# A new order of all work items in a two-layer attention and MLP kernel, and half of a matrix in other buffers

## The chip, the core and the metric

The kernel runs on one core of a Trainium2 chip. The core has TensorE (PE, matrix products into PSUM), VectorE (DVE), ScalarE (ACT), GpSimd (POOL) and SyncE (SP, which here issues nearly all DMAs). Each engine works through its own instructions in the order in which the program gives them; semaphores make an instruction wait for data of another engine or of a DMA. The metric is the device time of one execution in microseconds (us), lower is better.

## The reference

The input x is 2048 rows of 448 numbers in f32. Two layers follow each other with the same weights. Each layer is a linear attention block and an MLP block, both with a residual:

```
x = x + A(layernorm(x))          # twice, with B between and after
x = x + B(layernorm(x))

A: q, k, v = x @ wqkv            # 16 heads of 28
   phi(t) = (t + 1 if t > 0 else exp(t)) + 1e-6
   kv = sum over rows of phi(k) v     # per head, 28 x 28
   z  = sum over rows of phi(k)
   out = (phi(q) kv) / (phi(q) z + 1e-6) @ wo
B: gelu(x @ w1 + b1) @ w2 + b2   # 448 -> 1792 -> 448
```

## The kernel before

**Precision.** PE multiplies operands in a rounded format (fp32r). To keep f32 accuracy each operand is split in a high part and a low rest, and a product is made of three: high by high, high by low, low by high. This is why most matmuls come in threes, and why each operand costs a cast (ACT) and a subtraction (DVE or POOL). The last 64 of the 448 columns are packed so that they need two matmuls.

**Tiles and stages.** The rows are 16 tiles of 128. In a layer there are three stages.

*K, Q and G.* For each tile t: `ld` loads x, `a` takes the statistics (DVE), `ar` the root (POOL), `n` normalizes (DVE). The tile is transposed, either on PE (`T`, and `ht` in halves for the first two tiles) or by 32x32 blocks on DVE (`tu`), stored to HBM (`st`) and read back (`sp`), two tiles at a time. `xh` and `xl` split it. `K` and `Q` are 11 matmuls each. `ke`, `kp` apply phi to K (ACT, DVE), `kh`, `kl` split it, `za` adds it up for z (DVE); `qe`, `qp`, `qs` do the same for Q and store it to HBM. `sh`, `sl` split the normalized x as it is, and `G` (11 matmuls) adds up x by phi(k) over all tiles in four PSUM banks.

*From G to the MLP's input.* `z`, `zb`, `dc` make the denominator's vectors, `gt` copies G, `kv` multiplies it by the v weights, `mask` keeps the diagonal heads, and `m` multiplies by `wo`. The result M (448 x 448) is split by `mh`, `ml` in four groups of 112 rows. For each tile `pl` loads phi(q), `pz`, `pd`, `pm` divide it, it is transposed (`pT` on PE for the first four tiles, `pu`, `ps`, `pp` by way of HBM for the others), split (`qh`, `ql`) and multiplied by M: `o` for the first four tiles, `oc` after `mc` has moved M by 14 DMAs to the place of the q weights. `oa` adds it to x, and `la`, `ar`, `ln` normalize for the MLP; `mT` or `mu`, `ms`, `mp` transpose, `yh`, `yl` split.

*MLP.* The rows are four blocks of four tiles, the hidden 1792 columns 14 chunks of 128; a chunk of a block has the number n = 14 x block + chunk, 0 to 55. `f` is the first product of a chunk (11 matmuls of 512 columns), `g` the GELU (ACT), `gh`, `gl` the split (ACT, DVE), `y` the second product (12 matmuls of 448 columns, three for each of the block's tiles; `u` is one tile's three). `ya` adds the block's sums to x, and `ys` stores it.

The weights of the MLP are loaded piece by piece by `bld` and split by `bhi` (ACT) and `blo` (POOL) during the first layer; `wkld`, `wqld` load the k and q weights, `wkh` to `wql` split them, `wv` and `wo` load the v and output weights. `tab` is an ACT instruction on one number, and `fl` and `hot` are dummy matmuls whose result nobody reads.

**What sets the order.** Two long strings, `ORDER`, one for each layer, are a list of such items written out by hand or by a planner outside of this file. A name is followed by a number (tile, chunk or piece) and, behind a colon, an engine or a buffer ring if it isn't the usual one. `run` walks through the list and calls the function of each item, which emits its instructions at once; the compiler doesn't reorder them. So the list fixes the order on each engine and on each DMA queue. An item marked `>` belongs to the next layer, one marked `<` to the layer before: the layers overlap.

**Buffers.** PSUM has 8 banks: four `acc` (G, later the sums y), two `h` (Q, f) and two `m` (K and others). In SBUF the rings matter: `H`, 9 buffers of x; `S`, 5 buffers of 1024 numbers, for weights on their way, for transposes by way of HBM (`sq`, `sp`), for v and output weights and for M; `e`, 3 buffers, and `A`, `B`, 2 each, for the splits; `W0` to `W6` and `V0` to `V6`, one each, for the k and q weights and later for other things. Whoever takes a buffer of a ring waits until its last readers are done.

Lines in the profile: `copy` is L211, `hot` L228, `tab` L233, weight loads L246 to L258, transposes on PE L390, L465 and L737, on DVE L398 and L399, `st` L404, `sp` L410, `ld` L435, K and Q L543 to L548 (L489 to L497 for the first two tiles), phi L553 to L558, `kh` L576, `kl` L580, `za` L589, G L617 to L621, `oc` L785 to L789, f L850 to L854, `g` L859, `gl` L869, y L877 to L879, `ya` L896, `ys` L900.

Of the kernel before, what the change touches and what calls it, by code (L numbers as in the profile page):

```python
# [9 lines left out]
F32R = mybir.dt.float32r  # L10
AF = mybir.ActivationFunctionType
OP = mybir.AluOpType
# [55 lines left out]
    ),  # L68
    (
# [45 lines left out]
def linear_attn_mlp_kernel(  # L115
# [20 lines left out]
    G = 112  # L136
# [313 lines left out]
    @op  # L450
    def d(l, t, e):
        s = T["tail", l, t] = ring("tail", 128, "tail")
        copy(ENG[e or "a"], s.rearrange("p (u n) -> p u n", u=2),
             T["xn", l, t][:, None, TL:].to_broadcast([128, 2, 64]))
# [486 lines left out]
```

## Time and profile before

| what | before |
|---|---|
| time, median of 3 runs | 880.29 us (878.78 to 881.5) |
| span of the profiled execution | 878.3 us (no other time of it is recorded) |
| PE busy | 873.2 us, 99% of the span, 4181 matmuls |
| PE weight loads busy | 772.4 us |
| DVE busy | 473.7 us, 54% |
| ACT busy | 336.4 us, 38% |
| POOL busy | 202.6 us, 23% |
| granted PE clock | 1.000 |
| moved by DMA | 93.71 MB, mean 107 GB/s |

The profile is one execution, recorded by the hardware, and its times are counted from the start of the span. Matmuls are pipelined: one is shown as busy for 0.36 us, but the next starts about 0.20 us after it, so the distance from start to start is what PE's work costs, and a busy share of 99% doesn't by itself say how fast the products follow each other. A row of the timeline has the start, the duration, the engine, the line, the operation, what it writes and reads, and the shape; in brackets stands how long the engine had been idle before it, and what ended that. SPq and ACTq are DMA issues of these engines. A row of the groups has the count, the busy time in all and the mean of one in ns, and the idle time ahead of them.

### The profile page before, as it was taken

The page shows a single profiled execution, that of the slowest core. Times are in us where ns is not written, and L with a number is a line of the kernel's source. Part 1 is how long each engine was busy: PE and PEld are TensorE (multiplying, and loading weights), DVE is VectorE, ACT ScalarE, POOL GpSimd, SP SyncE. Part 2 cuts the span into 40 slices and gives each one's busy share as a digit, 9 for nine tenths or more (in the row PEclk, how much of TensorE's full clock was granted, in tenths as well). Part 3 has the DMA queues.
Part 4 walks back from the last instruction along what each step waited for, and adds up shares of the span by engine and source line. Part 5 has one row for each costly group of instructions (what it writes and reads, how often), then busy time and mean ns, then how long its engine had stood idle before and what let it go on. Part 6 is the DMA issues. An engine that isn't in the chain of part 4 may idle for free.

```text
span 878.3 us, 11548 instructions
## 1 busy us (share of the span) xinstructions
PE 873.2 (99%) x4181; PEld 772.4 (88%) x4181; DVE 473.7 (54%) x972; ACT 336.4 (38%) x596; POOL 202.6 (23%) x239
## 2 busy tenths in 40 slices
PE   9999999999999999999999999999999999999998
PEld 7999988889888888888899998988888888888887
DVE  7886587356574343324378765954572743343112
ACT  6777634332223221424355653333233132223221
POOL 4665543123132011010023333130220220130000
PEclk9999999999999999999999999999999999999999
DMA  6675732541613023221065452233125142120101
GB/s 210 175 234 171 222 95 98 159 130 58 213 58 117 30 82 103 78 84 49 24 206 160 138 182 85 94 124 99 65 88 166 46 119 84 39 96 5 38 1 43
DMA packets 62763, 93.71 MB, mean 107 GB/s; under 512 B 8817, under 2 KB 57969, under 8 KB 62705
## 3 DMA queue, kind: packets, MB, share of 16 engines
q1 hardware_dynamic: 62400, 92.51, 34.2%
q8 instruction: 33, 0.54, 0.3%
q10 hardware_dynamic: 304, 0.46, 0.2%
q14 instruction: 26, 0.20, 0.1%
HBM read 55.65 MB, written 34.08 MB: 102 GB/s over the span
## 4 chain that ended last, share of the span: by engine, by line
PE 99%; DVE 0%; ACT 0%; issue 0%; POOL 0%; POOLq 0%
PE y L878 10%; PE y L879 10%; PE y L877 10%; PE hp L851 9%; PE hp L852 9%; PE hp L850 9%; PE hp L854 3%; PE hp L853 3%; PE G L618 2%; PE psq L543 2%; PE G L617 2%; PE G L619 2%; PE psq L545 2%; PE psq L544 2%; PE psk L543 2%; PE psk L545 2%
## 5 line engine op out<-in xcount | busy, mean ns | idle before, releaser
L869 DVE TENSOR_TENSOR gl<-g,gh 128x512 fp32r<-128x512 f32 x112 | 79.8, 720 | 193.1 <-ACT gh L211 192.7
L878 PE MATMUL y<-w2l,gh 128*128 128x448 f32 x448 | 163.7, 365 | 0.0
L877 PE MATMUL y<-w2h,gh 128*128 128x448 f32 x448 | 163.6, 365 | 0.0
L879 PE MATMUL y<-w2h,gl 128*128 128x448 f32 x448 | 163.6, 365 | 0.0
L859 ACT ACTIVATE g<-hp,b1s 128x512 f32<-128x512 f32 x112 | 76.3, 688 | 227.8 <-PE hp L854 208.5
L851 PE MATMUL hp<-XH,w1l 128*128 128x512 f32 x336 | 131.2, 391 | 0.0
L852 PE MATMUL hp<-XL,w1h 128*128 128x512 f32 x336 | 131.1, 390 | 0.0
L850 PE MATMUL hp<-XH,w1h 128*128 128x512 f32 x336 | 131.1, 390 | 0.0
L211 ACT CAST gh<-g 128x512 fp32r<-128x512 f32 x112 | 69.1, 620 | 154.9 <-PE y L878 143.3
L357 POOL TENSOR_TENSOR brs<-bve,mhalf 128x1 f32<-128x1 f32 x64 | 41.0, 642 | 318.7 <-DVE bve L351 317.6
L877 PEld LDWEIGHTS y<-w2h,gh 128*128 128x128 f32 x448 | 84.1, 188 | 8.3
L878 PEld LDWEIGHTS y<-w2l,gh 128*128 128x128 f32 x448 | 84.1, 188 | 7.9
L879 PEld LDWEIGHTS y<-w2h,gl 128*128 128x128 f32 x448 | 84.1, 188 | 6.6
L852 PEld LDWEIGHTS hp<-XL,w1h 128*128 128x128 f32 x336 | 63.1, 188 | 13.6
L851 PEld LDWEIGHTS hp<-XH,w1l 128*128 128x128 f32 x336 | 63.1, 188 | 11.9
L850 PEld LDWEIGHTS hp<-XH,w1h 128*128 128x128 f32 x336 | 63.1, 188 | 11.8
L716 POOL TENSOR_TENSOR pz<-pq,zb 128x448 f32<-128x448 f32 x32 | 37.7, 1181 | 70.2 <-DVE dn L721 43.8
L535 POOL TENSOR_TENSOR xnl<-x,xnh 128x384 fp32r<-128x384 f32 x32 | 33.9, 1058 | 81.6 <-ACT xnh L211 81.2
L428 DVE TENSOR_TENSOR XL<-sp,XH 128x512 fp32r<-128x512 f32 x50 | 36.9, 752 | 22.7 <-ACT XH L211 22.5
L795 DVE TENSOR_TENSOR x<-op,x 128x448 f32<-128x448 f32 x32 | 19.8, 618 | 48.0 <-PE op L789 47.2
L853 PE MATMUL hp<-XH,w1x 128*128 128x512 f32 x112 | 43.6, 389 | 0.0
L854 PE MATMUL hp<-XL,w1x 128*128 128x512 f32 x112 | 43.6, 389 | 0.0
(162 smaller groups left out, 1573.1 us busy)
## 6 DMA issues: line engine op xcount, KB each, us to landing
x<-in_A_x_dram SPq DMA_DIRECT2D x32, 224.0 KB, 4.0
pq_d<-eq SPq DMA_DIRECT2D x32, 224.0 KB, 2.7
pq<-pq_d SPq DMA_DIRECT2D x32, 224.0 KB, 3.2
x<-x_d SPq DMA_DIRECT2D x32, 224.0 KB, 3.7
sq_a<-sq SPq DMA_DIRECT2D x13, 512.0 KB, 3.0
sp<-sq_a SPq DMA_DIRECT2D x52, 128.0 KB, 3.1
sq_q<-sq SPq DMA_DIRECT2D x12, 512.0 KB, 3.0
sp<-sq_q SPq DMA_DIRECT2D x48, 128.0 KB, 3.3
```

The source lines that it names most:

```text
L211: act.copy(out, src)
L357: pool.tensor_tensor(rs, ve, mhalf, op=OP.pow)
L850: pe.matmul(o, w1h[:, c, s], x.moving(x.hi, c), start=(c == 0), stop=False)
L851: pe.matmul(o, w1l[:, c, s], x.moving(x.hi, c), start=False, stop=False)
L852: pe.matmul(o, w1h[:, c, s], x.moving(x.lo, c), start=False, stop=False)
L853: pe.matmul(o, w1x[:, s], x.moving(x.hi, 3), start=False, stop=False)
L854: pe.matmul(o, w1x[:, s], x.moving(x.lo, 3), start=False, stop=True)
L859: act.activation(T[l, "g", n], T[l, "hp", n], AF.Gelu_apprx_tanh, bias=b1s[:, n % NF:n % NF + 1])
L869: dve.tensor_sub(lo, T[l, "g", n], f(hi))
L877: pe.matmul(o, gh[:, r], w2h[:, i, s], start=first, stop=False)
L878: pe.matmul(o, gh[:, r], w2l[:, i, s], start=False, stop=False)
L879: pe.matmul(o, gl[:, r], w2h[:, i, s], start=False, stop=last)
```

## The change

All 2,122 items of the two lists stay, each once as before; their order is new. Four new functions (`ac`, `kx`, `qx`, `nx`) are defined, and no item of the lists names them. In `mh`, the groups 0 and 1 of M take two buffers of the ring `S` (high and low part, two groups in a buffer), and the groups 2 and 3 take four buffers of the ring `H`, those of x; before, all four groups lay in four buffers of `S`.

In PE's part of the new order the first products f stand in 25 runs of one to seven chunks, against 72 runs of one to four before. The transposes on PE stand in 14 groups against 21. `fl` and `tab0`, which stood in the first stage, are the first two items. In the second list `tab0` and `wql3` come first, and more of the last chunks of layer 0 (marked `<`) stand in it. `wv1` is loaded early in the first stage of layer 0, and for layer 1 already during the MLP of layer 0.

```diff
 ORDER = (
     (
-        "ld0 a0 ar0 ld1 a1 n0 hot16 wkld0 wkld1:a wkld2 wkld3:a wkh1 wkl1 ht0 wkh0 ar1 wkl0 n1 d0 ht1 hx0 hl0 hk0 "
-        "wkh2 wkl2 wkh3 d1 ht3 hx1 hl1 wqld0 wqh0 ht2 hx2 wkl3:p hk1 hx3 hl2 hk2 hl3 wql0 hk3 ld2 wqld1 wqh1 a2 "
-        "ke0 kp0 bld1:xn wqld2 wqh2 wqld3 wqh3 kh0 sh0 wql2 wql3 wql1:p Q0 ar2 n2 d2 T2 sh1 sl0 kl0 G0 ld3 ld7 a3 "
-        "za0 qe0 qp0 xh2 xl2 ke1 ld4 ld9 a4 kp1 kh1 ld6 bld0:xn sl1 ar4 n4 za1 ar3 ld5 n3 d3 a5 qs0 bhi0 ar5 blo0 "
-        "Q1 qe1 K2 tab0 ke2 bld2:xn ld8 kl1 G1 T3 a7 qp1 n5 ar7 bhi1 blo1 kp2 a6 xh3 xl3 sh3 sh2 sl2 d4 kh2 Q2 T4 "
...
+        "tab0 fl ld0 a0 ar0 ld1 a1 wkld1:a wkld0 wkld3:a wkld2 hot16 wkh1 n0 wkl1 wkh0 d0 wkl0 ht0 hx0 wkh3 "
+        "wkh2 ht1 ar1 n1 d1 hl0 wkl2 hx1 wqld1 hk0 ld2 hl1 a2 wqh1 ht2 ht3 hx3 hx2 hl2 wqld0 wqh0 wkl3:p hk1 "
+        "wqld2 wqh2 ar2 hl3 ke0 hk2 ld10 hk3 n2 d2 T2 wql0 kp0 wqld3 wqh3 wql3 wql1:p wql2 Q0 kh0 ld6 kl0 sh0 "
+        "sl0 ld7 ld3 a3 ld5 a5 ar5 G0 xh2 ke1 xl2 kp1 bld1:xn bld0:xn bhi0 Q1 ar3 n3 bhi1 blo0 qe0 za0 sh1 sl1 "
+        "ld4 qp0 a7 d3 T3 xh3 za1 kh1 n5 d5 bld4:xn xl3 a6 K2 kl1 ar7 n7 blo1 ke2 wv1 bld3:xn ar6 bhi4 blo4 kp2 "
+        "qs0 qe1 a4 ar4 qp1 za2 Q3 G1 qe3 K3 kh2 qp3 T5 kl2 bhi3 n6 sh2 n4 d4 T4 sl2 tu7 a10 blo3 qs1 ld8 a8 "
...
     (
-        "ke0 Q0 K1 Q1 xh2 xh3 kp0 kh0 ke1 xl2 a5 ar5 xl3 n5 za0 tu5 qe0 <ys14 ld7 kl0 G0 a6 sh1 qe1 qp1 ld8 st2 "
...
+        "tab0 wql3 <gl53 st1 sp1 xh3 tu4 <f55 xh0 ld5 a5 xl0 <y53 xh2 xh1 xl2 K2 ar5 <gh54 xl1 xl3 n5 tu5 st2 "
+        "<g55 <gl54 <y54 <gh55 <gl55 ke2 K0 ke0 kp0 sp2 kp2 kh0 <y55 <ya14 kl0 <ya15 <ys15 xh4 xl4 <ya13 <ys13 "
...
+        "G5 n12 ar13 a14 tu12 kh6 kl6 n13 tu13 Q6 ar14 K7 ke7 n14 K8 kp7 za7 kh7 kl7 ke8 xh11 G6 kp8 xh10 K9 "
...
+        "G11 G12 ke13 kp13 qe9 za13 qp9 ld0 qs9 xh15 ld3 xl15 K15 kh13 sh13 sl13 ke15 kl13 sh15 xl14 K14 kp15 "
+        "ke14 kp14 pl1 kh15 sl15 kl15 ld1 qs6 G13 za14 Q8 za15 z sh14 kh14 zb sl14 kl14 G14 pl2 dc qe8 pz1 pd1 "
+        "qp8 pl3 pl0 pz0 pd0 pm1 G15 gt3 gt0 gt2 Q10 qe10 pT1 qs7 pz3 gt1 kv pd3 pm3 pl5 qp10 qs10 qh1 Q11 pz2 "
...
     @op
     def mh(l, g, e):
-        if g % 2 == 0:
-            T[l, "Mb", g // 2] = [ring("S", 1024, n, F32R) for n in ("Mh", "Ml")]
-        T[l, "Mh", g], T[l, "Ml", g] = (s[:G, g % 2 * D:(g % 2 + 1) * D] for s in T[l, "Mb", g // 2])
+        if g > 1:
+            T[l, "Mh", g], T[l, "Ml", g] = (ring("H", D, n, F32R)[:G] for n in ("Mh", "Ml"))
+        else:
+            if g == 0:
+                T[l, "Mb"] = [ring("S", 1024, n, F32R) for n in ("Mh", "Ml")]
+            T[l, "Mh", g], T[l, "Ml", g] = (s[:G, g * D:(g + 1) * D] for s in T[l, "Mb"])
         copy(ENG[e or "a"], T[l, "Mh", g], T[l, "mp", g])
```

More of the change, by code (lines that the diff above doesn't have):

```diff
@@ L450, in d, with ac, kx, qx @@
     @op
+    def ac(l, t, e):
+        xs = T["xn", l, t] = T["x", l, t]
+        st = small(6, "bst")
+        dve.bn_stats(st, xs)
+        mv = small(2, "bmv")
+        dve.bn_aggr(mv, st)
+        dve.tensor_scalar(xs, xs, mv[:, 0:1], None, op0=OP.subtract)
+        ve = small(1, "bve")
+        dve.tensor_scalar(ve, mv[:, 1:2], 1e-5, None, op0=OP.add)
+        T["st", l, t] = mv, ve
+    @op
+    def kx(l, t, e):
+        o = T["K", l, t]
+        act.activation(o, o, AF.Identity, scale=T["st", l, t][1])
+    @op
+    def qx(l, t, e):
+        o = T["Q", l, t]
+        act.activation(o, o, AF.Identity, scale=T["st", l, t][1])
+    @op
+    def nx(l, t, e):
+        xs = T["xn", l, t]
+        act.activation(xs, xs, AF.Identity, scale=T["st", l, t][1])
+    @op
     def d(l, t, e):
```

165 rows, old and new, of the table ORDER are left out of this document.

## The prediction

> **What bounds the kernel now.** I read the page first, then the chain of waits, then the timeline of TensorE matmul by matmul, because the first two leave nothing else to look for.
>
> ```profile
> span 878.3 us, 11548 instructions
> ...
> PE 873.2 (99%) x4181; PEld 772.4 (88%) x4181; DVE 473.7 (54%) x972; ACT 336.4 (38%) x596; POOL 202.6 (23%) x239
> ...
> PE 99%; DVE 0%; ACT 0%; issue 0%; POOL 0%; POOLq 0%
> ```
>
> PE is busy 99% of the span and is 99% of the chain. Both orders have the same 2,122 items, so the matmuls stay the same, and a new order can move four things: what PE loses before it runs without gaps, the waits inside, the rate at which a matmul follows the one before it, and the tail, whose four additions and stores keep their places. All of it is a few us. The sum is made against the profiled span, 878.3; no other time of that execution is recorded, and the runs' median, 880.29, is 2.0 above it (878.78 to 881.5). I carry that 2.0 over.
>
> **The change part by part.** *Runs of first products.* One chunk (f) is 11 matmuls of 512 columns. Timeline of PE in layer 0:
>
> ```profile
> 183.73 0.39 PE L850 MATMUL hp<-XH,w1h 128*128 128x512 f32 x1
> ...
> 186.25 0.36 PE L785 MATMUL op<-wq,qh 128*128 128x448 f32 x1
> ...
> 188.47 0.40 PE L850 MATMUL hp<-XH,w1h 128*128 128x512 f32 x1
> ...
> 190.99 0.39 PE L850 MATMUL hp<-XH,w1h 128*128 128x512 f32 x1
> ...
> 193.48 0.36 PE L877 MATMUL y<-w2h,gh 128*128 128x448 f32 x1
> ```
>
> The chunk at 183.73, behind a y, takes 2.52 us to the next item; the one at 188.47, behind an oc, also 2.52; the one at 190.99, behind another chunk, 2.49. So entering a run of chunks costs about 0.03 us. Read in this way at all 72 entries of the old order (the first at 139.69, the last at 867.25), it is 0 to 30 ns, mean 21, in sum 1.5 us; leaving a run shows no cost. In the new order PE's items have 25 such runs. Saved: 47 x 0.021 = 0.98 us. Bounds: 0 and 47 x 0.030 = 1.41.
>
> By the Trainium skill (TensorE: Matmul & The Clock Gate, Back-to-back issue gap) an isolated matmul of N columns needs N/2.4 + 2.5 ns, 215.8 ns at 512, whatever ran before. Here a chunk's follow each other in 2.49/11 = 226 ns, and the predecessor shows. By that rule this term would be 0; it stands below as a rival.
>
> The longer runs, up to 7 chunks, could make PE wait for its results to be cleared. Page, groups:
>
> ```profile
> L869 DVE TENSOR_TENSOR gl<-g,gh 128x512 fp32r<-128x512 f32 x112 | 79.8, 720 | 193.1 <-ACT gh L211 192.7
> ...
> L859 ACT ACTIVATE g<-hp,b1s 128x512 f32<-128x512 f32 x112 | 76.3, 688 | 227.8 <-PE hp L854 208.5
> ...
> L211 ACT CAST gh<-g 128x512 fp32r<-128x512 f32 x112 | 69.1, 620 | 154.9 <-PE y L878 143.3
> ```
>
> A chunk needs 0.69 + 0.62 us of ACT and 0.72 of DVE against 2.5 of PE, and ACT sits idle 227.8 us ahead of g, mostly waiting for PE's f. A run finds room for 2 chunks in the h banks, 3 in the ring e, and 2 in the rings A and B: 7, the longest run. The next y stands at least a chunk of PE work behind its own f in such a run, longer than 0.69 + 0.62 + 0.72 = 2.03. I count 0, hidden by PE's own work; without that cover a run would lose up to 2.03.
>
> *Transposes together* (21 groups become 14):
>
> ```profile
> 25.40 0.49 PE L390 MATMUL tp<-ident,x 128*128 128x128 f32 x3
> 25.73 0.27 PE L390 MATMUL tp<-ident,tail 128*128 128x128 f32 x1
> ...
> 26.04 0.36 PE L544 MATMUL psq<-wq,XH 128*128 128x448 f32 x1
> ```
>
> Three transposes take 0.33 up to 25.73, 0.11 each. From there to 26.04 lie the last one and the first product of a Q, 0.31, no more than a transpose (0.11) and a product (0.20, the 2.23 of eleven below) need alone. Nothing to save; bound 7 x 0.01.
>
> *The dummy matmul fl moves* from the middle of the first stage to the very start. Timeline, with two stretches of 11 products for the next point:
>
> ```profile
> 40.01 0.48 PE L228 MATMUL hot<-ones 128*128 128x512 f32 x1
> 40.33 0.37 PE L617 MATMUL G<-kh,xnh 128*128 128x448 f32 x1
> ...
> 44.86 0.37 PE L543 MATMUL psk<-wk,XH 128*128 128x448 f32 x1
> ...
> 47.14 0.37 PE L543 MATMUL psq<-wq,XH 128*128 128x448 f32 x1
> ...
> 90.29 0.36 PE L543 MATMUL psk<-wk,XH 128*128 128x448 f32 x1
> ...
> 92.52 0.36 PE L543 MATMUL psq<-wq,XH 128*128 128x448 f32 x1
> ```
>
> It took 0.32 there: saved. At the start it is a 17th dummy ahead of the first transposes: +0.23 (the spacing of 512 columns above) to +0.32; I take 0.24.
>
> *The rate in K, Q and G.* Eleven products took 2.28 us from 44.86 and 2.23 from 90.29, between 4 and 5 ns apiece more. The slow rate holds from just behind fl to about 88 us, and in short stretches later; over the 96 items it costs 1.6 us of a possible 96 x 0.05 = 4.8. What sets it the rows do not show (it ends and begins without a wait that I can see), so for the new order I keep 1.6: change 0, bounds -1.6 and +3.2.
>
> *The start.* Timeline, all engines:
>
> ```profile
> 0.80 0.41 ACTq L246 DMA_DIRECT2D stg<-in_A_wqkv_dram  x1
> 1.05 6.28 PE L228 MATMUL hot<-ones 128*128 128x512 f32 x16 [1.05 <-POOL ones L170]
> 2.43 1.28 ACT L211 ACT_TABLE_LOAD   x1 [2.43 <-issue]
> 4.24 0.56 ACT L211 CAST wk<-stg 128x448 fp32r<-128x448 f32 x1 [0.53 <-DMA stg<-in_A_wqkv_dram]
> 6.62 0.57 ACT L211 CAST wk<-stg 128x448 fp32r<-128x448 f32 x1 [1.82 <-DMA stg<-in_A_wqkv_dram]
> 7.58 0.37 ACT L211 CAST XH<-tp 128x256 fp32r<-128x256 f32 x1 [0.20 <-PE tp L465]
> 8.01 1.08 PE L489 MATMUL psk<-wk,XH 128*128 128x448 f32 x4 [0.24 <-ACT XH L211]
> 10.15 0.45 PE L493 MATMUL psk<-wk,XH 128*128 128x448 f32 x1
> ```
>
> ACT now issues three weight loads at 0.80 and loads its table while they fly. The new order opens with tab0, so the table (1.28) and tab0 itself stand ahead of those issues, and the first goes out near 2.3, 1.5 later. Behind it on ACT: the cast of that weight piece (4.24), then the cast of another piece, which waits for SP's load to 6.62 anyway, then the cast of the transposed x (7.58), for which the first K products wait. A landing 1.5 later, near 5.7, still lets the first cast end before 6.62. So the low bound is 0, the high one the whole 1.5; as there is only 0.3 us to spare and all loads share the same 16 DMA engines, I take 0.1, near the low end. SP's loads of x and weights change places among themselves; those that the first products need stay first, and the x tiles moved up are read later than the weights they pass. 0.
>
> *Waits inside.* PE in three places, with DVE once:
>
> ```profile
> 22.93 0.36 PE L617 MATMUL G<-kh,xnh 128*128 128x448 f32 x1
> 23.23 0.47 PE L618 MATMUL G<-kl,xnh 128*128 128x448 f32 x1
> 23.55 0.36 PE L619 MATMUL G<-kh,xnl 128*128 128x448 f32 x1
> ...
> 491.49 0.61 DVE L589 TENSOR_TENSOR za<-psk,za 128x448 f32<-128x448 f32 x1
> 491.85 0.37 PE L621 MATMUL G<-kl,xnh 128*128 128x448 f32 x1
> 492.25 0.44 PE L543 MATMUL psk<-wk,XH 128*128 128x448 f32 x1
> ...
> 535.08 0.37 PE L617 MATMUL G<-kh,xnh 128*128 128x448 f32 x1
> 535.40 0.47 PE L618 MATMUL G<-kl,xnh 128*128 128x448 f32 x1
> 535.72 0.36 PE L619 MATMUL G<-kh,xnl 128*128 128x448 f32 x1
> ```
>
> Each step above 0.20 is a wait for DVE: 0.21 us in G1 for kl1, 0.28 for the za that frees a bank of K (with the longer second matmul), 0.23 in G15 for kl15. In the new order kl1 has Q3 between it and G1, layer 1's za follow their kp at once or three items behind, and kl15 stands four PE items ahead of G15. All three go: -0.7. New ones are likely in the first 45 us, where the new order moves Q3, K3 and two tiles' transposes up on PE and so asks DVE for their operands sooner: bounds 0 and 2 (ten waits of this size); I take 0.4, two of them.
>
> *Half of M in buffers of x.* The same casts, subtractions and moves with other addresses. It frees 2 of 5 buffers of the ring S while M lives, and holds 4 of 9 buffers of x until the moves to the q weights' place are done, so later x loads wait; their x is first needed by oa4, behind four y of 2.4 us. 0. The four new functions are not named in the order and emit nothing.
>
> Sum: -0.98 - 0.32 + 0.24 + 0.1 - 0.7 + 0.4 = **-1.26 us**, 877.0 of span, **879.0**.
>
> **The rivals.** *All the slack goes.* Besides the terms above no new wait comes (-0.4) and, with fl gone from its place, the slow rate is not entered (-1.6): 879.0 - 2.0 = **877.0**. For it: the slow stretch begins at fl. Against: other stretches begin without one.
>
> *Entries cost nothing by themselves*, and the 21 ns go over to other places: 879.0 + 0.98 = **880.0**. Against it: chunks inside a run show 2.49 each time.
>
> *ACT's start is late in full.* tab0 ahead of the loads costs 1.5 rather than 0.1, and if the table that Relu picks lacks Exp, another 1.28 ahead of the first ek, K's way to G0: 879.0 + 1.4 + 1.3 = **881.7**. It decides from 1.4 of delay on, where it has used up the 1.26. By the Trainium skill (ScalarE: Activation LUTs, What ACT_TABLE_LOAD costs) a switch also drains for 1.38, and this would be 883.1; the row here has 1.28.
>
> *The ring S runs short.* By its place in the order wv1 is loaded after K2, near 22 us, and kept to the end of the stage (before: loaded after K15), and wv0 and wo1 follow after Q9 and Q8, which leaves 4, then 3 and 2 of the 5 buffers for the transposes by way of HBM. Page, issues, and the timeline:
>
> ```profile
> sq_a<-sq SPq DMA_DIRECT2D x13, 512.0 KB, 3.0
> sp<-sq_a SPq DMA_DIRECT2D x52, 128.0 KB, 3.1
> ...
> 485.65 1.74 SPq L410 DMA_DIRECT2D sp<-sq_a  x4
> ```
>
> With one pair of tiles at a time, a pair takes 3.0 + 3.1, 1.74 for four issues and about 4.4 of DVE and ACT (two turns, casts and subtractions), 12.2 in all, against 6 items x 2.23 = 13.4 of PE: hidden, by 1.2. If DVE's other work adds 2.2 to each pair, 1 us is lost on each of five pairs: 879.0 + 5 = **884.0**. It decides from a chain of 13.4 on.
>
> **How the numbers follow.** Chances: forecast 0.50 (879.0, its own range 877.7 to 880.6), all slack 0.21, entries 0.09, ACT's start 0.11, ring S 0.09. The range reaches to the cases on both sides, 876.4 to 882.4. With 0.3% (2.6 us) as the least that can be told from no change, faster means below 877.65: all slack and a little of the forecast, 0.22. Slower means above 882.9: ring S and the end of ACT's start, 0.11. Same: 0.67.
>
> **What would show it.** Runs of chunks: 2.49 inside, 2.52 at 25 entries. K, Q, G: 2.23 or 2.28 per item, and for how long. The first K product later than 8.01 by 0.2 to 0.4, with ACT's first issue near 2.3. No wait in G1, in K of layer 1 or in G15. The forecast is wrong if PE waits for more than 2 us in all behind its first product, or if the chain of waits shows another engine.

## The result and the profile after

The new order is slower. After took 886.43 us (median of 6 runs, 885.93 to 888.06), before, run beside it, 880.23 (878.78 to 882.0): ratio 1.0070, 95% interval 1.0057 to 1.0082. The prediction was 879.0, within 876.4 to 882.4.

The page of after: span, engines, and the shares of the chain of waits by engine.

```profile
span 884.6 us, 11556 instructions
...
PE 874.9 (99%) x4181; PEld 771.7 (87%) x4181; DVE 479.5 (54%) x972; ACT 338.2 (38%) x596; POOL 202.3 (23%) x239
...
PE 81%; DVE 6%; DMA 5%; ACT 3%; SPq 2%; issue 2%; POOL 2%; ACTq 0%; POOLq 0%; DVEq 0%
```

PE is "busy" 99% as before, but it was 99% of the chain and is 81% now; DVE, DMA, ACT, SP and POOL stand in most of the rest. Matmuls can't have become more; PE waits inside. Timeline of PE at four marks, after and then before: the first G, the first kv, the first f, the last product.

```profile
17.45 0.36 PE L647 MATMUL G<-kh,xnh 128*128 128x448 f32 x1
...
114.58 0.35 PE L693 MATMUL kvp<-gt,wvt 128*112 128x112 f32 x2
...
144.87 0.39 PE L883 MATMUL hp<-XH,w1h 128*128 128x512 f32 x1
...
880.62 0.37 PE L912 MATMUL y<-w2h,gl 128*128 128x448 f32 x1
```

```profile
16.16 0.45 PE L617 MATMUL G<-kh,xnh 128*128 128x448 f32 x1
...
111.19 0.26 PE L663 MATMUL kvp<-gt,wvt 128*112 128x112 f32 x1
...
139.69 0.39 PE L850 MATMUL hp<-XH,w1h 128*128 128x512 f32 x1
...
874.43 0.37 PE L879 MATMUL y<-w2h,gl 128*128 128x448 f32 x1
```

Up to G the new order loses 1.29 us, from G to kv 2.10 (97.13 against 95.03), from kv to f 1.79 (30.29 against 28.50), from f to the last product 1.01 (735.75 against 734.74). That is 6.2 of the 6.3, and 5.2 of it lies ahead of the first f, in the first sixth of the span.

The parts change from one execution to the next. In the nine profiles with before's list in the first stage (two of them with only `fl` moved) G to kv took 94.2 to 95.3 us, in the six with after's (one with only `tab0` moved) 95.7 to 99.3; kv to f took 28.4 to 28.5 and 29.5 to 30.3. From the first f to the last product before's list took 734.7 to 736.1 (before, `e5_fl`, `e18_mcfirst`), so the 1.01 behind the first f can't be told from this spread. PE's waits in after, by what ended them (us in total, times, longest):

```profile
PE op L820 <- DVE ql L431: 1.0, 1, 1.0
PE psk L573 <- DVE za L619: 1.0, 1, 1.0
PE kvp L693 <- DMA pq<-pq_d: 0.6, 1, 0.6
PE tp L393 <- DVE eq L588: 0.4, 1, 0.4
...
PE psk L575 <- DVE XL L431: 0.3, 1, 0.3
```

Each is a single event, ended by another engine. (The row of kv names a DMA of phi(q), which kv does not read; the weight load of the same product was released by DVE's copy of G, `gt`, at 115.47.) Measured from start to start against the usual step of their kind, all those above 0.1 us behind the first G come to 7.5 us, against 0.6 in before; 1.36 at oc4 (164.90 to 166.57), 1.2 at K (74.84) and 0.84 at kv (115.53) are the largest. The one at kv and two in the last transposes ahead of the first f (141.72 and 142.47, together 0.88) make the 1.79 between kv and f. With the 1.29 of the start that is 8.2 more, of which the entries of runs (1.1), the rate of K, Q and G (1.0) and fl (0.3) give back 2.4: 5.8 of the 6.2. Two waits can be read in the rows. K at 74.84, timeline of DVE and PE:

```profile
71.10 0.58 DVE L401 STREAM_TRANSPOSE sq<-x 128x384 f32<-128x384 f32 x1
...
71.79 0.65 DVE L431 TENSOR_TENSOR XL<-sp,XH 128x512 fp32r<-128x512 f32 x1
72.36 0.57 DVE L401 STREAM_TRANSPOSE sq<-x 128x384 f32<-128x384 f32 x1
...
73.55 0.61 DVE L610 SCALAR_TENSOR_TENSOR kl<-psk,kh 128x448 fp32r<-128x448 f32 x1
74.08 0.61 DVE L619 TENSOR_TENSOR za<-psk,za 128x448 f32<-128x448 f32 x1
...
73.50 0.37 PE L578 MATMUL psk<-wk,XL 128*128 128x448 f32 x1
74.84 0.44 PE L573 MATMUL psk<-wk,XH 128*128 128x448 f32 x1 [0.97 <-DVE za L619]
```

K10 needs the PSUM bank that za8 frees; in the new list za8 comes behind two transposes and a subtraction of other tiles on DVE (before it stood ahead of K9). And oc4, queue of SP, then the casts and PE; behind it the same part of SP's queue in before:

```profile
144.09 1.22 SPq L730 DMA_DIRECT2D wq<-Mh  x2
...
153.26 0.59 SPq L730 DMA_DIRECT2D wq<-Ml  x1
...
155.07 0.38 SPq L407 DMA_DIRECT2D sq_q<-sq  x1
158.78 1.75 SPq L413 DMA_DIRECT2D sp<-sq_q  x4
...
163.40 1.14 ACT L214 CAST qh<-sp 128x512 fp32r<-128x512 f32 x2 [3.02 <-DMA sp<-sq_q]
164.05 2.15 DVE L431 TENSOR_TENSOR ql<-sp,qh 128x512 fp32r<-128x512 f32 x2 [1.02 <-ACT qh L214]
164.59 0.47 PE L818 MATMUL op<-wq,qh 128*128 128x448 f32 x1
164.90 0.37 PE L819 MATMUL op<-wq,qh 128*128 128x448 f32 x1
...
166.26 0.47 PE L820 MATMUL op<-wq,ql 128*128 128x448 f32 x1 [0.99 <-DVE ql L431]
```

```profile
150.18 0.32 SPq L404 DMA_DIRECT2D sq_q<-sq  x1
152.81 1.74 SPq L410 DMA_DIRECT2D sp<-sq_q  x4
154.65 1.22 SPq L697 DMA_DIRECT2D wq<-Mh  x2
...
162.91 0.59 SPq L697 DMA_DIRECT2D wq<-Ml  x1
...
169.45 0.36 PE L785 MATMUL op<-wq,qh 128*128 128x448 f32 x1
```

In before the store and reload of the divided q go first and M's 14 moves second, and the first oc comes 29.8 us behind the first f. In after the moves go first and hold SP for 9.8 us, the reload is issued 6.0 us later, and the first oc comes only 19.7 us behind the first f: the two casts are done just in time for its first product at 164.59, and the third waits for ql, which is subtracted behind them.

### The profile page after: what moved, and what is told of

Read it like the earlier page. It is cut to its first block, busy times and chain, and to the rows that moved or that the text cites. A ratio compares the mean times of both kernels' runs of the same rounds, so it can differ in the third digit from the quotient of the medians.

```text
span 884.6 us, 11556 instructions
## 1 busy us (share of the span) xinstructions
PE 874.9 (99%) x4181; PEld 771.7 (87%) x4181; DVE 479.5 (54%) x972; ACT 338.2 (38%) x596; POOL 202.3 (23%) x239
## 4 chain that ended last, share of the span: by engine, by line
PE 81%; DVE 6%; DMA 5%; ACT 3%; SPq 2%; issue 2%; POOL 2%; ACTq 0%; POOLq 0%; DVEq 0%
PE y L912 10%; PE y L910 10%; PE y L911 10%; PE hp L885 8%; PE hp L883 8%; PE hp L884 8%; PE hp L887 3%; PE hp L886 3%; PE op L820 2%; PE op L819 2%; PE op L818 2%; PE psq L573 1%; PE psq L574 1%; PE psq L575 1%; DMA sq_a<-sq 1%
## 5 line engine op out<-in xcount | busy, mean ns | idle before, releaser
L350 DVE BATCH_NORM_STATS2 bst<-x 128x6 f32<-128x448 f32 x64 | 39.5, 617 | 10.3 <-DMA x<-x_d 5.0
L847 POOL TENSOR_TENSOR x<-x,b2b 128x448 f32<-128x448 f32 x32 | 40.8, 1284 | 10.2 <-DVE xm L364 6.9
```

Of the source, the lines that this page charges most:

```text
L847: (ENG[e or "p"]).tensor_tensor(T["x", l, t], T["x", l, t], b2b, op=OP.add)
```

## The experiments

Line numbers in the profiles of these kernels differ from after's by some lines. A time of "first f" or "kv" is the start of that row.

**tab0 behind the weight loads** (`e1_tab0`).

```diff
-        "tab0 fl ld0 a0 ar0 ld1 a1 wkld1:a ...
+        "fl ld0 a0 ar0 ld1 a1 wkld1:a ...
-   K2 kl1 ar7 n7 blo1 ke2 wv1 ...
+   K2 kl1 ar7 n7 blo1 tab0 ke2 wv1 ...
```

> The changed kernel with tab0 moved back from the very start to its old place in front of ke2 of layer 0; nothing else moved. In the changed kernel the first matmul of G0 starts at 17.45 us (before: 16.16), and ACT's first weight load goes out at 1.59 us instead of 0.80. Theory (the order of the casts and subtractions on ACT and DVE makes the start late, tab0 hardly matters, as the prediction priced it): G0 stays at 17.2 to 17.7. Rival (ACT's start is late in full because of tab0): G0 comes 0.8 us sooner, 16.4 to 16.9, and the span falls from 884.6 to about 883.8.

One run: 884.75 us (before beside it 879.95), span 883.0. The first G came at 17.36, so the place of tab0 is not what delays it. The span was 1.6 us shorter for another reason: kv came at 113.11, because the wait at K10 was not there in this execution.

**M's moves behind the reload** (`e2_mc`).

```diff
-   ... pm5 pu5 mc pu7 gl0 ... ps2 pp2 qh5 ...
+   ... pm5 pu5 pu7 gl0 ... ps2 pp2 mc qh5 ...
```

> The changed kernel with mc of layer 0 (14 DMAs that move M, 9.8 us of issues on SP's queue) moved from in front of ps2 and pp2 to behind them, their old order. In the changed kernel the first oc waits 1.15 us at 164.9 us for the tile that pp2 reads back. Theory (the wait is SP's queue, in which mc stands ahead of ps2): ql4 is ready some 9 us sooner, and the wait for it goes. Rival (another wait takes its place): M's moves now land last, near 168 us, and oc4 waits for them, 2 to 4 us, so that the span grows to 885.5 to 887.5.

One run: 890.42 us (before 879.95), span 888.7. oc4 had its ql in time, and now waited for M itself, 0.7, 1.0 and 0.8 us on three moves, with some ten products at half rate behind (what this half rate is stands in the last section). So with oc4 where it is, SP has too little time for both the moves and the divided q, in either order.

**Old first stage, and new first part** (`e3_oldfirst`, `e4_newfirst`): the one takes before's list up to Q15 of layer 0 and after's behind it, the other after's up to y13, the end of the first MLP block of layer 0, and before's behind it.

```diff
 e3: ... yh3 yl3 bhi25 blo25 pl5 pz5 Q15
+    blo24 bld28:W6 bhi28 lb1 bld27:W5 qs13 pd5 qs14 qe15 qp15 f2 ...
 e4: ... gl13 oc9 y12 yl7 yh4 y13
+    lb7 yl4 lb0 yl5 yl6 f14 g14 gh14 ya3 ya0 ya1 ys0 ...
```

> The old order up to and with Q15 of layer 0 (K, Q, G, M and the first four tiles' way to the MLP), then all other items in the new order; M of layer 0 lies in S as before, M of layer 1 half in H. Theory (the loss is made of waits in the first 145 us, where the changed kernel reaches the first f 5.2 us later, 144.9 against 139.7): span 884.6 - 5.2 = 879.4, within 1. Rival (the loss lies in what the new order does later, or in what both parts share, such as the buffers): span above 882.

> The mirror image: the new order up to and with y13 of layer 0 (its K, Q, G stage and the first block of the MLP), then all other items in the old order; M of layer 0 half in H, M of layer 1 in S. Theory (the loss is made in this part): 5.2 us up to the first f and about 1.1 in the first block, so a span of 878.3 + 6.3 = 884.6, within 1. Rival (the later part makes the loss): below 881.

e3: ratio 1.0094 (1.0079 to 1.0109); the first f came at 138.77, 6.1 us sooner than in after, but behind the joint one f waited 5.5 us: it needs a bank that Q15's phi frees, and qe15 stood on ACT behind the cast bhi28, which waited 6.1 us for its load. As a test of the rest it failed. e4: ratio 1.0069 (1.0052 to 1.0086), after's own loss, though all behind the first block is before's list. So the loss arises up to the end of that block. Its profile is of the longest of its four runs (888.79; the others 885.98 to 886.51): K10 waited 2.2 us, products behind it ran at half rate, and the first f came at 146.94; from there to the last product it took 736.2.

**Before's start in after's order** (`e10_start`): before's list up to G3, near 45 us.

```diff
 ... kl4 qs3 xl5 tu10 n11 a9 za4 tu8 G3
+wv1 ar9 n9 tu9 K5 bld6:xn bhi6 qe4 blo6 xh6 st4 ...
```

> The list of before up to its G3 in layer 0 (near 45 us), behind it all that is left in the order of after; M as in after. Theory A (each wait of the new order is a loss of its own): the later start of G (1.29 us) and the waits at T3, T4, G2 and Q2 (0.67, 0.21, 0.16, 0.34) go, 2.7 us in all: span near 882.0, ratio near 1.004. Theory B (the engines behind are late anyway, and an earlier start only meets the same operands later): the waits at 74 to 115 us grow by as much, and the span stays within 1 us of 884.6.

Ratio 1.0060 (1.0045 to 1.0075), against after's 1.0070 (1.0057 to 1.0082): no gain that can be told. Timeline of PE: the first G, and K10.

```profile
15.89 0.45 PE L658 MATMUL G<-kh,xnh 128*128 128x448 f32 x1
...
74.79 0.44 PE L584 MATMUL psk<-wk,XH 128*128 128x448 f32 x1 [2.01 <-DVE za L630]
```

G came 1.56 us sooner than in after, and the wait at K10 was 2.2 against 1.2, with 1.1 more at the joint; kv came at 114.17, near where it was (114.58). This is what theory B expected, and the 2.7 us of theory A did not come. That K10's wait grew because G came sooner is not shown: K10 waited 0.7 to 2.2 us in other executions of after's own list (see `e17_za8`).

**Before's front in after's order** (`e11_front`): before's list up to pd5, just behind the first f, with M in S in layer 0.

```diff
 ... qs13 blo24 f0 g0 gh0 pm4 lb1 pu4 pd5
+bld28:W6 bhi28 bld27:W5 f2 bhi27 g2 f3 pz7 f1 pd7 pm7 pm5 pu5 mc ...
```

> The list of before up to its pd5 in layer 0 (just behind the first f), behind it all that is left in the order of after; layer 0's M in four buffers of S as before, layer 1's as in after. Theory A (the loss lies ahead of the first f): the first f comes near 139.7 instead of 144.9, and the span is near 879.4, which is before's again; what stays is the wait of 1.36 us at oc4, against what the runs of f save. Rival C (the new order of the MLP and the four buffers of x lose as much as the front): the span stays over 882.

Ratio 1.0084 (1.0067 to 1.0101), no better than after. The first f came at 139.68, as before. Then, at oc4:

```profile
160.25 0.37 PE L928 MATMUL y<-w2h,gl 128*128 128x448 f32 x1
163.95 0.74 PE L834 MATMUL op<-wq,qh 128*128 128x448 f32 x1 [3.33 <-ACT qh L225]
...
165.72 0.74 PE L836 MATMUL op<-wq,ql 128*128 128x448 f32 x1 [0.65 <-DVE ql L442]
166.25 0.57 PE L834 MATMUL op<-wq,qh 128*128 128x448 f32 x1
166.63 0.57 PE L835 MATMUL op<-wq,qh 128*128 128x448 f32 x1
...
169.24 0.47 PE L899 MATMUL hp<-XH,w1h 128*128 128x512 f32 x1
```

PE got there 4 us sooner and waited: 3.5 us for qh, 1.0 for ql, and behind that eight products took 0.37 instead of 0.20, so that 6.6 us were lost at one place. The span is over 882, as theory C has it, but not for its reason: the gain of the front was taken back whole by the next chain.

**Cover for oc4** (`e9_f56`), and **both** (`e14_both`, the same move in e11_front).

```diff
-   ... qh4 ql4 y2 y3 oc4 pl9 f5 g5 qs15 ... oa4 la4 f6 g6 f7 ...
+   ... qh4 ql4 y2 y3 f5 f6 oc4 pl9 g5 qs15 ... oa4 la4 g6 f7 ...
```

> After with f5 and f6 moved on PE ahead of oc4, 5 us of products that need nothing of oc4's; nothing else moves. Theory A (oc4 waits because the store and reload of the divided q stand behind M's 14 moves on SP's queue, so it can be covered): the 1.36 us at oc4 go, and the span is near 883.3. Rival D (the divided q of the tiles behind is late by as much): the wait appears at oc5 or oc6 and the span stays near 884.6.

> The list of before up to its pd5 in layer 0 and behind it the order of after (as in e11_front), and now f5 and f6 stand ahead of oc4 on PE, 5 us of products. Theory A' (two chains set the loss one behind the other: first that of kv, which the front of before cures, then the divided q of oc4, which stand behind M's 14 moves on SP's queue; curing one alone meets the other): the waits of 3.5 and 1.0 us at oc4 and the slow matmuls behind them go, first f stays at 139.7, and the span is near 879.5, 1.2 above before. Rival C (the rest of the new order loses by itself): the span stays over 882.

e9: ratio 1.0060 (1.0038 to 1.0082); no wait at oc4 was left, and none came at oc5 or oc6, but its interval holds after's 1.0070, and its profile is of the shortest of four runs (883.82 to 888.07). e14: ratio 1.0011 (1.0002 to 1.0021), first f at 139.03, last product at 875.13. Page:

```profile
span 879.1 us, 11567 instructions
...
PE 92%; DVE 3%; DMA 2%; ACT 1%; issue 1%; POOL 0%; SPq 0%; DVEq 0%; ACTq 0%; POOLq 0%
```

This is the main result of the study. The front alone gained nothing (1.0084 against 1.0070), the cover alone 0.001, both together 0.006: two chains one behind the other, and the second takes whatever the first gives. What is left of the new order in e14 costs 0.0011 (0.0002 to 0.0021). In e11 and e14 layer 0's M lies in S as well; `e6_mS` below finds no difference in that.

**The loads of the output weights** (`e7_wv`): wv1, wv0 and wo1 behind K15 (before has wv1 and wv0 there, wo1 behind Q8).

```diff
-   ... blo1 ke2 wv1 bld3:xn ... bhi10 wv0 blo10 ... wo1 K11 ... K15 ...
+   ... blo1 ke2 bld3:xn ... bhi10 blo10 ... K11 ... K15 wo1 wv0 wv1 ...
```

> After with wv1, wv0 and wo1 of layer 0 loaded behind K15, as in before; nothing else moves. Rival S of the prediction (ring S is short of buffers from 22 us on): the waits of K near 74 and 98 us (1.2 and 0.56 us) go because the stores and reloads of transposed x start earlier, and kv comes at least 1.5 us sooner than 114.6. Theory A (no buffer is missing: those waits come at the end of a chain of loads of MLP weights, issues on SP and store and reload, which is as long without wv1): DMA durations of 4 to 5 us and waits of 0.5 us or more stay between 60 and 115 us, and kv comes within 1 us of 114.6.

One run: 894.41 us, span 892.7. K10 still waited (1.4 us) and kv came at 114.92, no sooner, so nothing here says that the ring S was short; but the wait near 98 us was not there in this execution. Then kv waited 5.2 us: the moved loads stood on SP ahead of three loads of phi(q), POOL waited 7.4 us for these, DVE's pd1 waited for POOL, and behind pd1 on DVE stood gt1, which kv needs.

**Earlier transposes by way of HBM** (`e15_tu`).

```diff
-   ... n4 d4 T4 sl2 tu7 a10 blo3 qs1 ld8 a8 xh5 G2 ... kh3 tu6 ... sl3 G3 st3 ...
+   ... n4 d4 T4 sl2 tu7 tu6 st3 a10 blo3 qs1 ld8 a8 xh5 G2 ...
...
-   ... ld9 a9 ar9 n9 tu9 K5 ... bld2:xn ld12 kh4 ... sp3 tu8 ... st4 ... K6 bld9:xn sp4 ...
+   ... ld9 sp3 a9 ar9 n9 tu9 tu8 st4 K5 ... bld2:xn ld12 sp4 kh4 ... K6 bld9:xn ...
```

> After with tu6, tu8 on DVE and st3, sp3, st4, sp4 on SP some 10 to 25 items sooner in layer 0 (tu6 behind tu7 and st3 behind it, sp3 behind ld9, tu8 behind tu9 and st4 behind it, sp4 behind ld12); PE's order stays. Theory T (the first stage is late because x transposed by way of HBM starts 4.5 us later than in before: first store at 37.9 instead of 33.4): the first store comes near 34 to 35, K's waits near 74 and 98 us (1.2 and 0.56) go, kv comes 1 to 2 us sooner than 114.6, and the waits at oc4 grow by as much, so that the span gains less, 883.0 to 884.6. Rival W (the loads of MLP weights and their splits hold ACT, POOL and DVE up): K still waits 0.7 us or more near 74 us, kv within 0.7 of 114.6.

Ratio 1.0172 (1.0158 to 1.0186). The edit made a new wait, and the rows show how (SP, DVE, PE):

```profile
34.22 0.33 SPq L418 DMA_DIRECT2D sq_a<-sq  x1
...
35.12 0.73 SPq L449 DMA_DIRECT2D x<-in_A_x_dram  x1
...
38.41 0.63 DVE L361 BATCH_NORM_STATS2 bst<-x 128x6 f32<-128x448 f32 x1 [3.30 <-DMA x<-in_A_x_dram]
...
40.09 0.47 PE L584 MATMUL psq<-wq,XH 128*128 128x448 f32 x1 [4.11 <-DVE XL L440]
```

The store now stood ahead of ld8 and waited for its transposes; the x behind it landed late; DVE waited in a8 for that x, with the operand of the next Q behind it, and PE lost 4.3 us to a tile that it needed much later. Theory T is left untested by this.

**DVE's order alone** (`e17_za8`).

```diff
-   ... K9 tu13 xl10 ar14 bld12:xn bhi12 tu12 qs6 ... qp7 kl8 za8 sl8 ...
+   ... K9 kl8 za8 tu13 xl10 ar14 bld12:xn bhi12 tu12 qs6 ... qp7 sl8 ...
```

> After with kl8 and za8 (which free the PSUM bank that K10 waits for near 74 us) on DVE right behind K9 in the list, ahead of xl10 and of the transposes tu13 and tu12; nothing else moves. Theory L (the wait is made by DVE's own order: two transposes and a subtraction of x stand ahead of the za that frees the bank): the wait of 1.2 us at K10 goes and kv comes 0.7 us or more sooner than 114.6. Rival H (DVE is late as a whole, and what passes is paid behind): the store st6 comes 1 us later than 74.4, K's wait near 98 us grows from 0.56 by as much, and kv stays within 0.4 us of 114.6.

Ratio 1.0049 (1.0034 to 1.0064), which overlaps after's 1.0070 (1.0057 to 1.0082). Timeline of PE: K10 begins without a wait, and behind it

```profile
73.20 0.36 PE L589 MATMUL psk<-wk,XL 128*128 128x448 f32 x1
73.40 0.37 PE L584 MATMUL psk<-wk,XH 128*128 128x448 f32 x1
...
96.59 0.37 PE L585 MATMUL psk<-wk,XH 128*128 128x448 f32 x1
97.64 0.47 PE L586 MATMUL psk<-wk,XL 128*128 128x448 f32 x1 [0.68 <-DVE XL L442]
```

the waits near 97 us rose from 0.56 to 1.2 (and 0.3 at 87). kv came 0.68 sooner, of which the first G had been ahead 0.20 and a faster rate of K, Q and G gave 0.24. So in this profile the wait is gone, as theory L has it, and most of it was paid back behind, as rival H has it. That the order of these DVE items made the whole wait is not shown by one profile: with after's own list up to there (and 1.1 in after, counted at its first product alone) K10 waited 0.7 us in `e6_mS`, 0.8 in `e9_f56`, 1.1 in `e2_mc` and 2.2 in `e4_newfirst`, and not at all in `e1_tab0`, where only tab0 had moved.

**M's moves first, in before** (`e18_mcfirst`).

```diff
-   ... pm6 ps2 pp2 mc bld26:W6 ...
+   ... pm6 mc ps2 pp2 bld26:W6 ...
```

> Before with the 14 moves of M (mc) on SP ahead of the store of the divided q (ps2) instead of behind its reload; nothing else moves. Theory E (the moves ahead alone cost nothing; it takes the early place of oc4 as well): the reload comes near 158 instead of 152.8 and lands near 162, its casts are done by 165, oc5 stays at 169.4 and the span within 0.5 us of 878.3. Rival M (the moves ahead of the divided q are the loss): oc5 or oc4 waits for ql, 1 us or more, span 879.3 and up.

Ratio 0.9996 (0.9987 to 1.0006). The reload was issued at 155.55, no oc waited. The moves ahead of the divided q cost nothing by themselves; with the first oc 10 us nearer to the first f they cost 1.4 to 6.6. This is theory E.

**Half of M in buffers of x** (`e6_mS`): after with before's `mh`.

```diff
-        if g > 1:
-            T[l, "Mh", g], T[l, "Ml", g] = (ring("H", D, n, F32R)[:G] for n in ("Mh", "Ml"))
...
+        if g % 2 == 0:
+            T[l, "Mb", g // 2] = [ring("S", 1024, n, F32R) for n in ("Mh", "Ml")]
```

> After with all four groups of M in four buffers of S, as before; the order stays that of after. Theory (the buffers of x that M takes cost nothing): 884.6 of span, ratio within 0.2% of after's 1.007. Rival (later loads of x wait for them and hold SP's queue up): 1 us or more less. Rival 2 (S is short with M in it): later loads wait, 1 us or more above.

Layer 0's and layer 1's M both lie in four buffers of S. Ratio 1.0062 (1.0048 to 1.0075) against after's 1.0070 (1.0057 to 1.0082): no difference that can be told. Its profile had a span of 883.3 and only 0.2 us of wait at oc4, whose reload came 1.3 us sooner; one profile can't say whether the buffers do that.

**The last MLP alone, and fl** (`e12_late`, `e13_latefl`, `e5_fl`): before's list up to pm4 of layer 1 and after's behind it; the same with fl at the start; before with fl at the start.

```diff
 e12, e13: ... pz5 pd5 pm5 pm4
+    f2 f1 g1 lb3 pz7 u2 u3 pd7 mc u1 u0 ...
 e13, e5:
-        "ld0 a0 ar0 ...
+        "fl ld0 a0 ar0 ...
```

> The list of before up to its pm4 in layer 1 (the first f of layer 1), and only behind it the order of after: the runs of f of the last MLP alone; M in four buffers of S in both layers. Theory (an entry of a run of f costs 21 ns, as the prediction has it): from the first f of layer 1 to the last product 0.5 to 0.6 us less than the 303.2 of before, span near 877.8. Rival (entries cost nothing by themselves): 303.2 as before, 878.3.

> As e12_late, and the dummy product fl stands at the start instead of in the first stage of layer 0. Theory (fl is what starts the slow rate of K, Q and G): besides the 0.1 us of the move itself, about 1 us less between G0 and kv, span near 876.7. Rival (the slow rate comes by something else): 0.1 us less than e12_late, near 877.7.

> Before with the dummy product fl moved from the first stage of layer 0 to the start, and nothing else; M in four buffers of S. Theory (fl starts the slow rate): no stretch of 2.28 us for eleven products behind 40 us, and span near 877.2. Rival: the slow stretch is there as before, span near 878.2.

e12: ratio 0.9998 (0.9989 to 1.0007).

From the first f of layer 1 (571.34) to the last product (874.30) it took 302.96 us, 0.20 less than before. Read as in the prediction, the entries of runs cost 0.94 us in all at 49 entries, against 1.50 at 72, so the 23 entries gave 0.56; a new wait of 0.22 for gl in a run, and smaller losses, took most of it. Over all profiles after's list took 302.55 to 303.39 us there (after itself 302.56) and before's 303.16 to 303.28. e13: 1.0000 (0.9991 to 1.0010); e5: 1.0001 (0.9992 to 1.0011). fl does not set the rate. Groups of K's first product between 41 and 88 us, in e18_mcfirst, where fl stands in its old place, and in e5_fl, where it stands at the start:

```profile
L584 PE MATMUL psk<-wk,XH 128*128 128x448 f32 x24 | 8.8, 365 | 0.0
```

```profile
L584 PE MATMUL psk<-wk,XH 128*128 128x448 f32 x24 | 8.8, 369 | 0.0
```

365 ns is the fast rate and 369 the slow one. Between G and kv the slow rate cost 1.03 us in before, 1.28 in e12, 0.07 in e18 and 0.07 in e16, all with the same list there: it belongs to the execution, not to the order.

**A version for more** (`e16_best`): e14_both with two weight casts of ACT later, for which f1 waited 1.34 us in it.

```diff
-   ... bld28:W6 bhi28 bld27:W5 f2 bhi27 g2 f3 ... gh1 gl1 u3 ...
+   ... bld28:W6 bld27:W5 f2 g2 f3 ... gh1 gl1 bhi28 bhi27 u3 ...
```

> As e14_both, and the casts of two MLP weight pieces on ACT, bhi28 and bhi27, stand behind gl1 instead of ahead of g2, for which f1 waited 1.34 us. Theory A' (nothing else of the new order loses): that wait goes, and the span is near 877.8, 0.5 below before, of which the runs of f give about 0.9. Rival: the wait only turns into one of the same size behind it, span near 879.

Ratio 1.0011 (1.0002 to 1.0020), span 879.1, as e14_both. That wait went, and 0.9 us came back in PE's next item, where a y waited for gl. The rival held. No version here beats before.

## Why the prediction was wrong, step by step

- *Waits inside: new ones +0.4, bounds 0 and 2.* This is the step that failed: new waits were put at 0.4 us, and behind the first G they are 7.5. The three old waits went as predicted. The bound was drawn as "ten waits of this size" in the first 45 us, from waits that DVE showed in the old order. Such a row prices a wait that is there; it says nothing of how late a moved item may become. What the rows show ahead of the operands that came late is the order on DVE and SP: which item stands in front of the one that PE needs (za8 behind two transposes; ps2 behind 14 moves). That was to be read in the diff, list against list.
- *Half of M in buffers of x, "the same casts, subtractions and moves": 0.* The buffers may well be 0 (e6_mS). But the place of `mc` changed in the order, and its 14 issues on SP's queue, 9.8 us, were not counted though the step says "moves". Together with oc4's earlier place it is 1.36 us in after, 6.6 with a faster front.
- *The start: +0.1; "SP's loads ... 0".* ACT's first issue went out at 1.59, not near 2.3, and the first K product started at 7.83, sooner than before. The first G was 1.29 later all the same, by waits for ACT (the copy of tile 1's tail, behind casts of k weights) and DVE (x of tile 2, a q weight). Wrong in size and in what came late; e10_start found no effect on the end that can be told.
- *Runs of f: -0.98.* Right: 1.50 us at 72 entries, 0.44 at 25 in e17_za8, which has after's runs, 18 to 21 ns an entry. The formula of the Trainium skill (TensorE: Matmul & The Clock Gate, Back-to-back issue gap), by which this term would be 0, is for an isolated matmul; it does not fit these rows, in which the predecessor shows. But "the next y stands at least a chunk of PE work behind its own f", which made the long runs free, fell short in places: y waited for gl 0.22 us in e12, 0.44 in e10 and 0.45 in e17.
- *fl: -0.32 + 0.24, and the rate: change 0, bounds -1.6 and +3.2.* The bounds were sound and the reason offered for the gain (the slow stretch begins at fl) is refuted by e5 and e18. In after the slow rate cost 1.0 less than in before. That is luck of the execution: other executions of before's list show it as well.
- *Transposes together: 0.* No row contradicts it.
- *The rivals.* "The ring S runs short", 884.0, came nearest in time, but no run shows its cause (in e7_wv kv came no sooner). "ACT's start is late in full": with tab0 back in its place the first G was as late (e1_tab0), and the drain that its 883.1 adds did not show at a table switch: in before one took from 443.51 to 444.79 and the next activation began at 444.80. "Entries cost nothing by themselves": they cost 18 to 21 ns each. "Wrong if PE waits for more than 2 us, or if the chain shows another engine": both happened.
- *Sum:* its gains were there (1.1 for the entries, 0.6 for the old waits); the loss that it lacked is 1.2 at the start (1.29 against 0.1) and 7.1 of new waits behind it (7.5 against 0.4).

What stays open: which moves in the front make its loss (e11 and e14 show only that before's front, with cover for oc4, takes it away), and why K10's wait ranges from 0.7 to 2.2 us between executions that have the same list up to there.

## What to carry to other kernels

When a list of items is reordered and the bound engine is busy 99%, don't price the change on that engine: go down the new order of each *other* in-order engine and queue, and for each operand PE needs ask what now stands ahead of it (transposes ahead of the op that frees a bank, 14 DMA issues, 9.8 us in all, ahead of a store and reload). Stalls in a row do not add: curing the first alone gave nothing (1.0084), the second alone 0.001, both 0.006, so an experiment that cures one suspect and shows no gain has not cleared it. And a store issued earlier on a queue that waits in order delays every load behind it (e15_tu, 1.7%).

## What the runs showed of the hardware

After a long wait the granted clock of PE falls to half for a few microseconds, which the mean of a run hides (0.996 in e11_front). The stretch behind the wait at oc4 in e11_front, by the view of stretches of time: start and end, length, PE busy and its matmuls, granted clock, busy share and GB/s of the DMA engines.

```profile
162.57:169.40 6.83, 4.80 (x12) 0.50 0.06 22
```

Behind the 3.5 and 1.0 us of waits eight products of 448 columns in a row took 0.37 us each instead of 0.20, so that stalls of 4.5 us cost 6.6. The traces have the clock at 0.5 for 6.83 us at the waits of 5.5 us in e3_oldfirst and 5.2 in e7_wv too, and for 3.41 us behind 2.2 us in e4_newfirst, behind 4.3 and again behind 2.65 in e15_tu, and behind three waits of 0.7 to 1.0 within 3 us in e2_mc, but not behind the 2.2 us in e10_start. The Trainium skill (TensorE: Matmul & The Clock Gate, Part 1: The HAM clock gate) names a free-running window of about 3.4 us without work as what halves the clock; the 3.41 and 6.83 us fit one and two such windows, but here the half clock also came behind shorter waits. In after's six runs the two with a mean granted clock of 0.998 are the longest, 887.19 and 888.06 us, against 885.93 to 886.47.

The two rates of K, Q and G (365 and 369 ns a record, 0.203 and 0.207 us from start to start) change between executions of one list, worth up to 1.3 us: of the size that this change was predicted to bring.
